# Wider first loads, a split last tile, and a re-weighted list schedule in a sparse attention and mixture-of-experts kernel

## The chip, the cores and the metric

One core of a Trainium2 chip runs the whole kernel. The metric is device time in microseconds (us) of one execution; less is better. Before the change the kernel took 168.26 us (median of three runs, 168.03 to 168.26). Engines are called PE (TensorE), VectorE (DVE in the profile), ScalarE (ACT), GpSimd (POOL) and SyncE (SP).

A profile has one execution and lists a span, which is some 1.6 us shorter than the time of the same execution (164.5 and 166.12 us in the kernel before). Each run carries a state, fast or slow. On one core "slow" means only that the run was more than 1.5% above the fastest run of the same kernel.

## The reference, cut to what matters

Four batches of 768 rows with eight heads of 64 columns go through a sparse attention (a window of 16 positions on each side, and 24 block summaries). The result, pooled over its rows, picks one of eight experts per batch; all rows of the batch then go through that expert's two layers. The code is shortened.

```python
def _attn_ref(q, k, v):                       # 4 x 8 x 768 x 64
    k_sum = k.reshape(B, H, nb, 32, D).max(axis=3)
    v_sum = v.reshape(B, H, nb, 32, D).mean(axis=3)
    scores_l = scale * q @ k.T                # kept where |i - j| < 16
    scores_s = scale * q @ k_sum.T + log(32)
    a = softmax(concat([scores_l, scores_s]))
    return a @ concat([v, v_sum])

def _moe_ref(x, w_gate, w1, w2):              # x: 4 x 768 x 512
    logits = x.mean(axis=1) @ w_gate
    e_idx = np.argmax(logits, axis=1)         # ONE expert per batch
    ...
    h = np.maximum(x[mask] @ w1[e], 0.0)      # 512 -> 1024
    out[mask] = gate_w * (h @ w2[e])          # 1024 -> 512
```

What matters is the chain of dependences: no expert weights can be loaded for a batch before all of its attention is done and its gate has been evaluated. For batch 0 this chain stands alone at the start of the program.

## The kernel before

The kernel is written as a list of operations with assumed durations. A list scheduler (`Plan`) runs over them when the program is built, gives each a start time, an engine and buffers, and then emits the instructions in that order. At each step it takes, from the operations that could start within 0.03 us of the earliest, the one with the least priority number.

```python
class Plan:
    LAT = {"pe": 0.27, "act": 0.1, "dve": 0.1, "pool": 0.1, "q": 1.6, "sp": 0.1}
    def solve(self):
        # ... for each operation whose dependences are placed: earliest start, engine, buffers
                found.append((pick[1], op.prio, op.idx, pick[0], pick[2], op, ats, room))
        # ...
            st, _, _, end, eng, op, ats, room = min(
                (c for c in found if c[0] <= smin + 0.03), key=lambda c: (c[1], c[2]))
            op.spare = st - max(room, free.get(eng, 0.0))
```

Two helpers give PE products of zeros to do at the start. `first_warm` is the first thing that PE does; `warm` puts fillers in front of an operation that the plan has waiting. They are meant to keep PE's clock up.

```python
    def warm(op, tile_):
        if op.start < WARM_UNTIL:                    # 60 us
            for _ in range(int((op.spare - 0.1) / 0.17)):
                nc.tensor.matmul(tile_, lhsT=zb[:, 0:128], rhs=zb[:, 0:HB], ...)

    def first_warm(op):
        ps = one_pool.tile([128, 512], FP32, name="wps", ...)
        for _ in range(9):
            nc.tensor.matmul(ps, lhsT=zb[:, 0:128], rhs=zb, start=True, stop=True)
```

The attention of a pair of heads is, on PE: transposes of k and q (`tps`), the scores of a half pair (`sc`, 12 to 16 small matmuls), the block sums of v (`vsps`), the product with v (`ops`), and the transpose of the result (`xps`). There is a single score buffer (`"sc": 1`). The gate's matmul is `lgps`; the expert's layers are H (`hps`) and Y (`o_ps`). The first loads, and the order of the later ones:

```python
    loads_kq(0, "k", [0], 0.8, KQ)                   # one pair of heads: 192 KB
    R["ident"] = add(("pool", 1.7), constants, 0, [last[0]])   # identity and four iotas
    for pr in ALLP:
        if pr:
            loads_kq(0, "k", [pr], 0.7, KQ)
        loads_kq(0, "q", [pr], 0.7, KQ)
        if pr == 1:
            loads_v(0, [0, 1], 2.2, VV)
    loads_v(0, [2, 3], 2.2, VV)
    # ...
    ORDER = ["kq1", "v1", "w0", "kq2", "v2", "w1", "kq3", "v3", "w2", "w3"]
```

`kq1` and `v1` are batch 1's inputs, `w0` is batch 0's gate with the loads of its expert's weights.

The softmax here doesn't subtract the row's maximum and nothing guards it: scores larger than these inputs give would overflow.

## Time and profile before

| Kernel before | Value |
|---|---|
| median of 3 runs | 168.26 us |
| profiled run | 166.12 us, span 164.5 us, mean PE clock 0.957 |
| first H matmul (steady PE work begins) | 44.99 us |
| last PE work ends, last store lands | 160.28 us, 163.11 us |

Note that the profiled run was 2 us quicker than the timed ones of the same kernel.

### The profile page before, as it was taken

The numbers are of one execution on the slowest core, as the hardware profiler recorded it, in microseconds if no ns is written. First come the engines' busy times: TensorE is split into PE (matmuls) and PEld (weight loads), VectorE is DVE, ScalarE is ACT, GpSimd is POOL, SyncE is SP. The second block draws the span as 40 slices with busy tenths as digits, with TensorE's granted clock in tenths as the row PEclk, the third lists the DMA queues.
The fourth block names the chain that finished last, engine by engine and source line by source line (L and its number), as shares of the span: only waits on it lengthen the run. The fifth ranks groups of instructions, "written<-read, shape, count | busy, mean of one in ns | idle before, by whom it ended". The sixth has DMA issues, their size and how long they took to land.

```text
span 164.5 us, 5002 instructions
## 1 busy us (share of the span) xinstructions
PE 148.9 (91%) x2136; PEld 88.0 (53%) x2136; DVE 96.9 (59%) x264; ACT 99.7 (61%) x199; POOL 46.5 (28%) x63
## 2 busy tenths in 40 slices
PE   6986989952999999999999999999999999799990
PEld 2445856741666666546556656457565445355440
DVE  5892997794498878776987588549963101000000
ACT  3174584983278766975867678469675435653341
POOL 6998600007950000697000046000000280000000
PEclk9996599995599999999999999999999999999999
DMA  3999999999999999999999999999500099990333
GB/s 32 128 137 187 164 176 210 161 133 91 162 189 206 209 176 138 102 135 262 255 234 207 194 149 144 249 257 248 113 0 0 35 165 194 277 213 12 128 128 128
DMA packets 60037, 26.01 MB, mean 158 GB/s; under 512 B 42608, under 2 KB 56944, under 8 KB 60016
## 3 DMA queue, kind: packets, MB, share of 16 engines
q0 software_dynamic: 56032, 19.40, 130.3%
q1 hardware_dynamic: 3984, 6.31, 11.3%
q8 instruction: 16, 0.26, 0.7%
q14 instruction: 5, 0.04, 0.1%
HBM read 38.81 MB, written 6.29 MB: 274 GB/s over the span
## 4 chain that ended last, share of the span: by engine, by line
PE 65%; DMA 15%; POOL 6%; DVE 6%; issue 4%; ACT 1%; POOLq 0%; ACTq 0%
PE hps L661 23%; PE o_ps L689 19%; DMA vblk<-in_v_dram 8%; DMA w_sb<-in_moe_w_dram 7%; PE tps L355 5%; PE sc L481 4%; PE ops L511 4%; PE xps L543 3%; PE vsps L426 2%; DVE vblk L447 2%; POOL k_nat L191 2%; POOL q_nat L191 1%; POOL vblk L202 1%; PE vsps L722 1%; DVE kmx L383 1%
## 5 line engine op out<-in xcount | busy, mean ns | idle before, releaser
L661 PE MATMUL hps<-xT,w_sb 128*128 128x384 bf16 x256 | 47.7, 327 | 1.4 <-DMA w_sb<-in_moe_w_dram 1.4
L689 PE MATMUL o_ps<-w_sb,hT 128*128 128x512 bf16 x192 | 44.4, 380 | 0.0
L623 POOL DMA_DIRECT2D w_sb<-in_moe_w_dram x16 | 12.0, 763 | 85.8 <-DVE kaug L402 37.8
L496 ACT ACTIVATE aT<-sc 128x768 bf16<-128x768 f32 x32 | 25.9, 808 | 11.8 <-PE sc L481 11.7
L680 ACT ACTIVATE hT<-hps 128x384 bf16<-128x384 f32 x45 | 22.1, 491 | 15.1 <-PE hps L661 14.9
L661 PEld LDWEIGHTS <-w_sb 128*128 128x128 bf16 x256 | 22.8, 98 | 15.1 <-DMA w_sb<-in_moe_w_dram 2.2
L689 PEld LDWEIGHTS <-hT 128*128 128x128 bf16 x192 | 17.4, 98 | 19.6
L708 ACT ACTIVATE o_sb<-o_ps,gcol 128x512 f32<-128x512 f32 x22 | 15.1, 687 | 16.2 <-PE o_ps L689 13.4
L528 DVE TENSOR_TENSOR xs<-ops,rv 128x384 bf16<-128x384 f32 x32 | 17.8, 558 | 1.1
L678 DVE TENSOR_SCALAR hT<-hps 128x384 bf16<-128x384 f32 x19 | 10.6, 556 | 12.1 <-PE hps L661 12.0
L552 ACT ACTIVATE xT<-xps 128x384 bf16<-128x384 bf16 x32 | 15.6, 491 | 1.2 <-PE xps L543 1.0
L202 POOL DMA_DIRECT2D vblk<-in_v_dram x10 | 15.8, 1587 | 1.4 <-DMA w_sb<-in_moe_w_dram 1.0
L481 PE MATMUL sc<-qT,kaug 64*128 64x64 bf16 x384 | 12.1, 198 | 4.6 <-issue 2.6
L317 DVE TENSOR_TENSOR aT<-aT,seen 96x768 bf16<-96x768 bf16 x24 | 12.9, 546 | 4.0 <-ACT aT L496 4.0
L383 DVE TENSOR_REDUCE kmx<-kaug 128x24 bf16<-128x768 bf16 x16 | 14.8, 932 | 0.3 <-ACT kaug L365 0.3
L365 ACT COPY kaug<-tps 128x768 bf16<-128x768 bf16 x13 | 10.0, 795 | 7.8 <-PE tps L355 7.8
L481 PEld LDWEIGHTS <-kaug 64*128 64x128 bf16 x384 | 8.3, 99 | 10.8 <-issue 7.5
L447 DVE COPY vblk<-vs_sb 24x1536 bf16<-24x1536 bf16 x16 | 12.1, 753 | 2.6 <-ACT vs_sb L365 2.2
L543 PE MATMUL xps<-identb,xs 128*128 128x128 bf16 x96 | 10.7, 220 | 0.6 <-DVE xs L528 0.6
L365 ACT COPY qT<-tps 128x768 bf16<-128x768 bf16 x13 | 9.9, 798 | 2.1 <-PE tps L355 2.0
L511 PEld LDWEIGHTS <-aT 120*64 120x64 bf16 x384 | 8.4, 117 | 5.0 <-issue 3.4
L511 PE MATMUL ops<-vblk,aT 120*64 120x65 bf16 x384 | 10.4, 203 | 0.3 <-DVE vblk L447 0.3
(89 smaller groups left out, 145.8 us busy)
## 6 DMA issues: line engine op xcount, KB each, us to landing
w_sb<-in_moe_w_dram POOLq DMA_DIRECT2D x12, 512.0 KB, 13.4
out_dram<-o_sb SPq DMA_DIRECT2D x24, 256.0 KB, 5.9
vblk<-in_v_dram POOLq DMA_DIRECT2D x6, 576.0 KB, 22.2
k_nat<-in_k_dram POOLq DMA_DIRECT2D x3, 768.0 KB, 14.5
q_nat<-in_q_dram POOLq DMA_DIRECT2D x3, 768.0 KB, 17.6
vblk<-in_v_dram POOLq DMA_DIRECT2D x2, 564.0 KB, 18.4
w_sb<-in_moe_w_dram POOLq DMA_DIRECT2D x8, 128.0 KB, 4.5
w_sb<-in_moe_w_dram POOLq DMA_DIRECT2D x4, 256.0 KB, 7.7
```

Of the source, the lines that this page charges most:

```text
L202: nc.gpsimd.dma_start(vb[p0:p1, n0:n1, 0:D], bass.AP(v.tensor, v.offset + ((b * H * NJ + n0) * QB - HALO + p0) * D, [[D, p1 - p0], [QB * D ...
L365: nc.scalar.copy(out_, in_)
L383: nc.vector.tensor_reduce(out=kmxs[b, pr].rearrange("q (j c) -> q j c", c=QB // BLK), in_=kaugs[b % 2][:, pr, :, R_OWN:R_POST].rearrange(" ...
L481: nc.tensor.matmul(sc[:, hh, w * QB : (w + 1) * QB], lhsT=ka[rs, pr, j, :], rhs=qT[rs, j * QB : (j + 1) * QB], start=b > 0 and w == 0, sto ...
L496: nc.scalar.activation(aT, scs.pop((b, pr, u))[:, :, 0:HB], ACT.Exp, scale=SCALE)
L511: nc.tensor.matmul(ops[w * QB : (w + 1) * QB, t, hh, :], lhsT=aT[0:NR, hh, c0 : c0 + QB], rhs=vb[0:NR, 2 * pr + hh, u * NW + 2 * t + w, 0 ...
L528: nc.vector.tensor_tensor(out=xs, in0=ops[:, :, :, 0:D], in1=rv.unsqueeze(3).to_broadcast([128, NW // 2, 2, D]), op=ALU.mult,)
L543: nc.tensor.transpose(xps[:, t * 128 : (t + 1) * 128], xs[:, t], identb)
L552: nc.scalar.activation(xT[b][:, pr, u * HB : (u + 1) * HB], xpss.pop((b, pr, u)), ACT.Copy, accum_out=red[b][:, pr, u : u + 1],)
L661: nc.tensor.matmul(hps[:, 0:HB], lhsT=w1_sb[:, dt, ft * 128 : (ft + 1) * 128], rhs=xT[b][:, dt, u * HB : (u + 1) * HB], start=(dt == 0), s ...
L680: nc.scalar.activation(dst, hps[:, 0:HB], ACT.Relu)
L689: nc.tensor.matmul(o_ps, lhsT=hTs[b][:, ft, st * 128 : (st + 1) * 128], rhs=wts[b][1][:, ft, :], start=(ft == 0), stop=(ft == NFT - 1),)
```

## The change

The intent has three parts. (1) *Loads*: batch 0's k and q come in four transfers of two pairs of heads instead of eight of one, v last, and the identity is built early, apart from the other constants. (2) *Halves*: the last 128 rows of the output are computed, evicted and stored as two halves of 256 columns, so that what follows PE's last matmul is shorter. (3) *Plan*: urgencies per kind of operation are added to the priorities, found by a search in which the model's durations were disturbed; and the plan gets a term for the fetching of PE's instructions, a block of 256 usable `FETCH` us after the block before was entered.

```diff
+    FETCH = 4.5
+    SLACK = 0.03
+    URGENCY = {
+        "Vs": 3, "gb": 155, "mul": 100, "vo": -37, "xo": -99, "qo": 4, "Tq": 4,
+        "kmx": 7, "S": -20, "rest": -4, "exp": -120, "own": -113, "X": 6, "H": 152,
+        "ho": 152, "gc": 152, "Y": 152, "yo": 152,
+    }
     ... [solve; the rest of it keeps a list of ready operations, with the same choice]
+                if op.count:
+                    r = max(r, come.get((done + op.count) // block, 0.0))
-                found.append((pick[1], op.prio, op.idx, ...
+                found.append((pick[1], op.prio + self.URGENCY.get(op.kind, 0.0), op.idx, ...
+            if op.count:
+                if (done + op.count) // block > done // block:
+                    come[(done + op.count) // block + 1] = end + self.FETCH
+                done += op.count
     ... [halves]
+    def Z_mm(b, st, c):      # o_ps[:, 0:256] = hT x w2[:, c-th half], 8 matmuls
+    def Z_out(b, st, c):     # evicts 256 columns and issues its own store
-        for st in range(NST):
+        for st in range(NST - (b == B - 1)):
+        if b == B - 1:
+            for c in range(2):
+                ...
+                m = add(("pe", 0.9), Z_mm(b, NST - 1, c), "Y", base + 20 + c, ...)
+                o = add(EITHER(0.45, 0.5), Z_out(b, NST - 1, c), "yo", base - 165, [m, gc])
     ... [loads]
+    FIRST = "k01 i0 q01 k23 i1 q23 v01 v23".split()
-    loads_kq(0, "k", [0], 0.8, KQ)
-    ... [the loop shown above]
+    for what in FIRST:
+        if what[0] == "i":
+            R["ident", int(what[1])] = ... (identity, constants)[int(what[1])] ...
+        elif what[0] == "v":
+            loads_v(0, [int(c) for c in what[1:]], 2.2, VV)
+        else:
+            loads_kq(0, what[0], [int(c) for c in what[1:]], 0.7, KQ)
     ... [every add() gets a kind; PE's also a count of instructions; the plan's time for a v load goes from 2.15 to 2.25]
```

The arithmetic is unchanged.

## The prediction

> **What bounds the kernel now.** The program runs on one core, so I went straight to the page's 40 slices, then summed three stretches, then read the chain of waits and the waits list. Slices (each 4.1 us; tenths of a slice) first:

> ```profile
> PE   6986989952999999999999999999999999799990
> PEclk9996599995599999999999999999999999999999
> DMA  3999999999999999999999999999500099990333
> ```

> From slice 12 on TensorE (PE) is full, at full clock, but for one dip near slice 35; before that it is patchy, and its granted clock falls twice. The sums (columns: stretch, length, then busy us and count per engine, clock, DMA share, GB/s):

> ```profile
> 0.00:44.50 44.50, 34.86 (x687) 23.08 (x689) 32.27 (x99) 24.93 (x44) 23.93 (x39) 0.85 1.85 143
> 44.50:160.00 115.50, 113.80 (x1464) 64.88 (x1452) 64.59 (x165) 73.91 (x154) 22.53 (x25) 1.00 1.30 166
> 160.00:164.50 4.50, 0.28 (x2) 0.00 (x0) 0.00 (x0) 0.88 (x2) 0.00 (x0) 0.94 0.31 117
> ```

> So three regimes: 44.5 us of start, 115.5 us in which PE is busy for 113.8, and 4.5 us of tail. In the middle the order of instructions can gain almost nothing except the idle 1.7 us. The waits list names most of it, and the other stall that matters:

> ```profile
> PE sc L481 <- issue: 2.6, 1, 2.6
> PE hps L661 <- DMA w_sb<-in_moe_w_dram: 1.4, 1, 1.4
> ```

> The second is the last batch's first weights, late at 144.1. The first lies in the start; the chain of waits shows where (columns: start us, length, what):

> ```profile
> 10.76 13.98 DMA vblk<-in_v_dram
> 24.78 0.86 PE vsps L426 x24
> ...
> 34.97 0.35 PE lgps L576 x8
> ...
> 35.43 0.23 PE sc L481 x4
> 35.67 2.64 issue
> 38.31 0.41 PE sc L481 x8
> ```

> The start hangs on the second half of batch 0's v, landed at 24.74 (10.76 + 13.98), then on 10 us of attention work up to the gate's matmul (lgps, 34.97), then on the gate's weights. Those are issued at 37.88 and land from 42.30. The last v of batch 1 landed at 40.14, just ahead of them: in this trace the loads land nearly in issue order, so the weights stand behind 1.5 MB of k and q and 1.15 MB of v of batch 1. Steady PE work begins at 44.7 to 45.0.

> [...]a fetch packet starts at 35.38 and takes 1.54 us, and PE stands still from 35.67 to 38.31 with nothing to wait for. I read this stall as that fetch; no run yet proves it. [...]the records show 0.5 from 13.7 to 20.6, after the thin stretch 11 to 15, and again from 37.6 to 44.5, right after the stall. [...]The last six stores of 256 KB land 2.0 us after issue[...].

> **The change part by part.**

> First loads. Eight issues of one pair of heads (192 KB; k and q, four pairs) become four of two pairs (384 KB), and the eye matrix is built before the four iotas instead of with them. GpSimd pays 0.63 us for each such issue (median of the k_nat and q_nat rows early on), so 4 x 0.63 = 2.5 us less. Today k0's 192 KB are alone in the queue from 2.24 to 4.59, when q0's issue ends: the engines have little to do until then. After, 384 KB are queued by 2.3, the next 384 KB by about 3.6 (0.6 us of identity plus 0.75 us of issue). v's two halves go to the end, issued at about 6.4 to 8.8 and 8.8 to 10.6. The bytes before the end of batch 0's v are the same 2.7 MB, only fed sooner: I take 2 us (between 1.5 and 2.7) off v's last landing, 24.7 to about 22.7, and off everything behind it: batch 1's last v from 40.1 to about 38. The first half of v lands later (15.0 today, about 17 to 19 then), the k and q of pairs 2 and 3 much earlier (15.6 to 19.5 today, about 10 to 12 then). That is a good exchange: scores need k and q only, eight of them fit the nine aT buffers, and so ScalarE's 8 x 0.81 us of exp and 8 x 0.80 us of copies can be done before the last v. The first transpose starts later (384 KB in place of 192 KB at some 190 GB/s: +1.0 us on 5.34) but is not on the path: VectorE's constants occupy it to 6.8 today and set the first maximum.

> The last rows. The last 128 rows go as two halves of 256 columns: 16 matmuls instead of 8. Three transposes of 128 columns with their weight loads take 0.17 us, 0.056 each, so 256 columns should take 0.11: 16 x 0.11 = 1.76 us against 8 x 0.218 = 1.75. PE breaks even. The last eviction, 0.69 us for 512 columns, falls to about 0.45 (384 columns take 0.49), and the store loses perhaps 0.2 of its 2.0. Sum: -0.4 us, all on the path.

> Urgencies, slack and the fetch model. They change no arithmetic, only order, ScalarE or VectorE, buffers and the fillers[...]. H, Y and their evictions fall by 152, that is behind the attention of the next two batches, which so ends earlier; the gate of the last batch follows, and with it the last weights: I count half of the 1.4 us wait, -0.7. The model spreads PE's instructions so that a block of 256 is not used up within 4.5 us of its fetch. If that removes the 2.64 us stall, the half clock after it goes too. What it is worth: steady work could begin when the first weights land. They are issued after attention 0 (about 2 us sooner from v, about 1 more from less VectorE and ScalarE work left after v) and must land behind batch 1's v (about 38): at 40 to 41 instead of 42.3, and PE takes them at once rather than at 45.0. Steady work begins up to 4 us earlier; I count 3, as the fillers and a new order will not hit it exactly. Against this +0.2 us for stalls at new places.

> Sum: -3.0 - 0.7 - 0.4 + 0.2 = -3.9 us of 168.26, to 164.4 us.

> **The rivals.** (a) *The weights' landing sets the steady start.* If DMA is saturated from 6 us on whatever the order (its row shows 9 in slices 2 to 28), the loads gain only their first idle microsecond, and the change is worth 1 + 0.7 + 0.4, about 2 us: 166.2. For: the row of nines. Against: today PE starts 2.7 us after the weights are there. (b) *Fetch stalls move.* Drawn together, attention uses 24 or 32 instructions per 0.3 to 0.45 us, a block in some 4 us; today's late fetch cost more than the modelled 4.5 us[...]. Two new stalls of 2.6 us with half clock after them eat the gain: 168 to 169. Against: the search has this term, and today's steady stretch shows no such gap. (c) *All of it works*: weights at 39, four more score groups done before them (4 x 0.28), no wait for the last weights: -6 -1 -1.4 -0.5 with some loss, 160 to 161. For: ScalarE and VectorE are busy only 25 and 32 us of the first 44.5. Against: such plans meet real durations that the model has not.

> **Range and chances.** Rival (a) at 166.2 and the full success at 160.5 lie on both sides of 164.4; the profiled run of before took 166.1 and the timed ones 168.0 to 168.3, so the start varies by 2 us on its own. Range 160.8 to 167.4. The 2% line is 164.9, close to my centre: faster 0.57, within 2% 0.40, slower 0.03, since nothing adds work to the saturated middle.

> **What would show it.** Right: k and q of all pairs landed by 12 to 13 us; batch 0's v by 23; the gate's matmul at 31 to 33; no PE issue gap over 1 us in the first 45 us, and no half clock after 21; first H matmul at 40 to 42; the busy sum of the steady part unchanged within 2 us; the last eviction at 0.45 us; the wait for the last weights under 0.7. Wrong: v's landing unmoved (then rival a), a new issue gap followed by clock 0.5 (rival b), or PE idle between the early attention and the weights, which would say that landing alone sets the start.

## More of the kernel before

From the profile's costliest groups (busy us, mean ns of one, idle before) and its table of queues (packets, MB, share):

```profile
L661 PE MATMUL hps<-xT,w_sb 128*128 128x384 bf16 x256 | 47.7, 327 | 1.4 <-DMA w_sb<-in_moe_w_dram 1.4
L689 PE MATMUL o_ps<-w_sb,hT 128*128 128x512 bf16 x192 | 44.4, 380 | 0.0
q8 instruction: 16, 0.26, 0.7%
```

The two layers alone are 92 us of PE work, which no order of instructions makes smaller.

## The result, and the profile after

| | before | changed |
|---|---|---|
| runs | 168.26, 168.03, 168.26, 167.20 | 165.29, 165.71, 165.48, 165.85 |
| median | 168.14 us | 165.59 us |
| profiled run: time, span | 166.12, 164.5 us | 165.29, 163.6 us |

The ratio is 0.986 (95% interval 0.982 to 0.990), within the 2% that counts as the same. A ratio is the mean time of one kernel's fast runs over the mean of the other's of the same rounds, so it is not quite the ratio of the medians quoted. A repetition on another chip (below, after_again) gave 0.996 (0.990 to 1.003). So the two estimates of the gain are 1.4 and 0.4%, and the second is not clear of nothing.

The same views as the prediction read, for the changed kernel: the slices, then the three stretches (cut at the same 44.5 and 160 us).

```profile
PE   6797789694498999999999999998999999999991
PEclk9999999759569999999999999999999999999999
DMA  2999999991999999999999999999500099993333
```

```profile
0.00:44.50 44.50, 33.73 (x662) 22.22 (x663) 33.44 (x101) 24.43 (x44) 19.32 (x32) 0.88 1.97 133
44.50:160.00 115.50, 114.18 (x1486) 66.23 (x1480) 67.06 (x168) 72.40 (x151) 25.03 (x28) 0.99 1.34 170
160.00:163.60 3.60, 0.02 (x1) 0.00 (x0) 0.00 (x0) 0.47 (x1) 0.00 (x0) 0.99 0.32 114
```

The dip near slice 35 is gone, and the stretch after 160 us is 0.9 us shorter (PE's own end came 0.26 us of that sooner). But the start is as long as it was: PE is full from slice 12 on, no sooner, and the low clock has moved, from slices 4 to 5 and 10 to 11 to slices 8 to 9 and 11 to 12. The chain of waits through the start of the changed kernel (start us, length, what) says why:

```profile
28.77 0.18 PE ops L537 x4
28.95 1.62 issue
30.57 0.43 PE ops L537 x8
...
32.86 1.39 PE xps L780 x4
...
35.22 2.08 PE tps L381 x47
37.30 0.02 issue
37.32 0.96 DVE qT L393
...
40.01 0.36 PE sc L507 x12
```

The stall of 2.64 us that stood at 35.67 in the kernel before has become one of 1.62 us at 28.95, in the middle of a group of 12 matmuls that had begun, with nothing to wait for. It no longer stands behind the gate but in front of it. Then come four fillers (L780), and batch 1's transposes, the last 64 of them of q, and only then the gate's matmul, at 37.58 instead of 34.97. The records give the half clock from 30.39 to 37.22 and from 40.63 to 47.46. Two stretches of 3.41 us, each just before such a fall, from the sums by stretch of the changed kernel (length, then PE's busy time and count first; the clock is third from the end):

```profile
26.98:30.39 3.41, 1.97 (x64) 1.48 (x54) 2.50 (x6) 2.55 (x6) 0.00 (x0) 1.00 2.17 169
30.39:33.80 3.41, 3.23 (x47) 2.29 (x48) 2.51 (x4) 1.27 (x3) 0.00 (x0) 0.50 4.35 136
37.22:40.63 3.41, 1.54 (x50) 1.10 (x47) 3.24 (x12) 2.43 (x6) 0.31 (x1) 1.00 0.09 8
```

A 3.41 us stretch in which PE was busy for 1.97 us was followed by half clock; so was one with 1.54. In the first, all the idle time is the stall. (The half clock of each of these two falls lasted 6.83 us, and so it did at the two falls of the kernel before in its start; a stretch is half of that, and the full clock between the changed kernel's two spells lasted just 3.41 us.) But so short a stall was not always followed by half clock. I cut all 14 traces into such stretches, in step with the clock's own changes: of those at full clock, every one with PE busy for less than 1.8 us was followed by half clock (18 of the 25 falls), and none with more than 2.3 us was. Between these it went either way: in before_shift128, 33.01 to 36.42 us with 1.82 us busy was not followed by half clock, and 36.42 to 39.83 with 2.30 was.

**Where the time of the profiled pair went.** I counted PE's useful work, each kind of matmul at the time that it takes at full clock, fillers left out: 123.4 us in all. (The times per kind are my estimate from the traces; with other reasonable ones the total is up to 128 us, and one kernel shifts against another by 0.2 to 0.5 us. Smaller differences of this count are not to be read.) The first 16 us of it are done at 44.31 us before and at 44.51 after. So the start gained nothing. At 30 us of useful work the changed kernel is 1.9 us behind (61.50 against 59.63; its first layers ran at half clock to 47.46), at 60 us of it 1.0 behind, at 104 us of it 1.5 behind. Only then, where the wait for the last batch's weights stood, does it catch up, making good 1.75 us: at 122 us of work it is 0.3 ahead. The tail, from PE's end to the last landing, is 2.83 us before and 2.33 after. Net: 0.77 us between the last landings (163.11 and 162.34). The timed difference of 2.5 us is larger because the profiled run of before was one of its quick ones.

### The profile page after: what moved, and what is told of

The parts are those of the page before. It is cut to its first block, busy times and chain, and to the rows that moved or that the text cites. A ratio compares the mean times of both kernels' runs of the same rounds, so it can differ in the third digit from the quotient of the medians.

```text
span 163.6 us, 5016 instructions
## 1 busy us (share of the span) xinstructions
PE 147.9 (90%) x2139; PEld 88.5 (54%) x2139; DVE 100.5 (61%) x268; ACT 97.3 (59%) x196; POOL 44.3 (27%) x59
## 4 chain that ended last, share of the span: by engine, by line
PE 79%; DVE 10%; ACT 3%; DMA 3%; issue 2%; ACTq 0%; POOLq 0%
PE o_ps L715 25%; PE hps L687 25%; PE tps L381 8%; PE xps L569 4%; PE sc L507 4%; PE ops L537 4%; DVE vblk L473 4%; DMA k_nat<-in_k_dram 3%; PE vsps L452 2%; PE tps L780 2%; ACT aT L522 2%; DVE qT L393 1%; DVE kmx L409 1%; PE o_ps L744 1%; PE xps L780 1%
## 5 line engine op out<-in xcount | busy, mean ns | idle before, releaser
L715 PE MATMUL o_ps<-w_sb,hT 128*128 128x512 bf16 x184 | 43.5, 380 | 0.0
L687 PEld LDWEIGHTS <-w_sb 128*128 128x128 bf16 x256 | 23.5, 98 | 13.4 <-issue 0.5
L706 ACT ACTIVATE hT<-hps 128x384 bf16<-128x384 f32 x44 | 21.2, 490 | 12.1 <-PE hps L687 11.6
L715 PEld LDWEIGHTS <-hT 128*128 128x128 bf16 x184 | 16.4, 98 | 17.7
L734 ACT ACTIVATE o_sb<-o_ps,gcol 128x512 f32<-128x512 f32 x19 | 13.1, 687 | 16.2 <-PE o_ps L715 12.9
L343 DVE TENSOR_TENSOR aT<-aT,seen 96x768 bf16<-96x768 bf16 x24 | 12.3, 550 | 4.1 <-ACT aT L522 4.0
L537 PE MATMUL ops<-vblk,aT 120*64 120x65 bf16 x384 | 9.8, 198 | 3.4 <-DVE vblk L473 1.8
L391 ACT COPY kaug<-tps 128x768 bf16<-128x768 bf16 x11 | 8.4, 797 | 6.3 <-PE tps L381 6.3
L473 DVE COPY vblk<-vs_sb 24x1536 bf16<-24x1536 bf16 x16 | 11.6, 725 | 0.7 <-ACT vs_sb L391 0.3
L537 PEld LDWEIGHTS <-aT 120*64 120x64 bf16 x384 | 7.9, 112 | 7.0 <-issue 4.2
```

Source lines behind the costliest of these rows:

```text
L391: nc.scalar.copy(out_, in_)
L473: nc.vector.tensor_copy(vblks[b % NV][R_SUM:NR, 2 * pr : 2 * pr + 2, :, 0:D], vss[b, pr][BLK * pr : BLK * pr + NB] .unsqueeze(2) .to_broad ...
L537: nc.tensor.matmul(ops[w * QB : (w + 1) * QB, t, hh, :], lhsT=aT[0:NR, hh, c0 : c0 + QB], rhs=vb[0:NR, 2 * pr + hh, u * NW + 2 * t + w, 0 ...
L687: nc.tensor.matmul(hps[:, 0:HB], lhsT=w1_sb[:, dt, ft * 128 : (ft + 1) * 128], rhs=xT[b][:, dt, u * HB : (u + 1) * HB], start=(dt == 0), s ...
L706: nc.scalar.activation(dst, hps[:, 0:HB], ACT.Relu)
L715: nc.tensor.matmul(o_ps, lhsT=hTs[b][:, ft, st * 128 : (st + 1) * 128], rhs=wts[b][1][:, ft, :], start=(ft == 0), stop=(ft == NFT - 1),)
```

## The experiments

All kernels gave correct results. "Mark" is the time at which the first 16 us of useful PE work are done. "before" in a row of times means the kernel before, run in the same rounds. By the 2% rule no run has a verdict other than "same" or "unclear" on record (unclear: after_again, gate_first, hold_v1 and shift256; none for shift128). So what follows rests on the intervals and, above all, on the traces.

### The parts one at a time

Theory A: the loads and the plan act on the start and each gives a part of the gain. Rival B: the start is set by when PE's instructions come, so the parts show nothing there, and what remains is the tail and the last weights.

**halves_only**: the kernel before with the halves alone.

```diff
-        for st in range(NST):
+        for st in range(NST - (b == B - 1)):
...
+        if b == B - 1:
+            for c in range(2):
+                ... Z_mm and Z_out as in the change, no urgencies
```

> The kernel before plus only the two half stores at the end; its first 150 us are the same instructions, so its trace is also a second look at the start of the kernel before. Tail theory: the span loses the 0.7 to 0.8 us that the last landing moved (163.11 to 162.34 in the two traces), so the time is 0.5 to 0.8 us under the kernel before, ratio 0.995 to 0.997. Rival: sixteen matmuls of 256 columns cost PE what the smaller store saves, ratio 0.999 to 1.001. Its start should show a PE issue gap at recorded instruction 1217 (mod 256 = 193) if the gap is the instruction fetch.

Measured: 166.55 us median (165.45 to 167.92) against 166.84 for before (11 runs, four of them slow), ratio 1.002 (0.996 to 1.009). From PE's end to the last landing it took 2.34 us, not 2.83. The stall in the start is where it was, from PE's part of the timeline (start, length, engine line op; in brackets the idle time before):

```profile
38.09 0.40 PE L481 MATMUL sc<-qT,kaug 64*128 64x64 bf16 x8 [2.42 <-issue]
```

So the halves are worth 0.5 us at the end of the trace, too little to show in six runs that scatter over 2.5 us: the times decide for neither expectation. The stall is at 1217, as expected.

**loads_only**: the kernel before with the new first loads alone.

```diff
-    loads_kq(0, "k", [0], 0.8, KQ)
-    ... [old loop]
+    FIRST = "k01 i0 q01 k23 i1 q23 v01 v23".split()
+    for what in FIRST: ... [as in the change]
```

> The kernel before plus only the two-pair first loads and the split constants; no urgencies, no halves. Theory A (loads move data 2 us sooner, but instruction fetch and the half clock after it hold the gate back): the last v of batch 0 lands at 22 to 23, yet the gate's matmul stays at 33 to 37 and the time gains 0 to 1.2 us (ratio 0.993 to 1.000). Rival B (the loads are the gain): ratio 0.982 to 0.988, as the whole change.

Measured: 166.28 us (165.60 to 167.26), ratio 1.000 (0.995 to 1.006). Batch 0's last v landed at 23.5 instead of 24.74 and batch 1's at 38.72 instead of 40.14, so the data came 1.2 and 1.4 us sooner. PE did not profit. Its timeline:

```profile
35.87 0.29 PE L578 MATMUL lgps<-wg_sb,reds 128*1 128x8 f32 x6 [0.24 <-DVE reds L569]
39.21 0.19 PE L578 MATMUL lgps<-wg_sb,reds 128*1 128x8 f32 x2 [3.05 <-issue]
44.95 1.46 PE L663 MATMUL hps<-xT,w_sb 128*128 128x384 bf16 x4
```

Here the stall cuts the gate's own eight matmuls in two, so that the first weights land only at 44.78 (42.30 before). Steady work begins at 44.95, as before. In this order the weights' landing does come just ahead of the steady start.

**no_urgency**: the changed kernel with `URGENCY = {}`.

```diff
-    URGENCY = {"Vs": 3, "gb": 155, ...}
+    URGENCY = {}
```

> The whole change without the table of urgencies (empty), so with the new first loads, the halves and the fetch term. Theory A (what the whole change gains after the start comes from the urgencies, by the last batch's weights being issued or needed at a better time): the PE wait for the last weights is back at 1 us or more, and the time is 0.8 to 2 us over the whole change (ratio to before 0.991 to 0.998). Rival B (loads and halves carry it all): ratio 0.984 to 0.988, wait or not.

Measured: 166.12 us (165.17 to 166.41), ratio 0.997 (0.992 to 1.002). A stall of 3.57 us ended at 38.88, with the gate's matmul behind it. The time is in the range of Theory A, but its mechanism, that the wait for the last batch's weights comes back, was a miss. PE's last H work has no such wait:

```profile
140.81 5.39 PE L683 MATMUL hps<-xT,w_sb 128*128 128x384 bf16 x32
```

The wait is 1.4 us in the kernel before, 1.3 in halves_only and 1.0 in before_shift128; it is 0 in the changed kernel, 0.39 in after_again, and 0 in loads_only (less than 0.05) and old_first too. So in these traces, one of each, it went with the new loads under the old plan and with the urgencies under the old loads; the urgencies are not needed for it.

**old_first**: the changed kernel with the old order of the first loads.

```diff
-    FIRST = "k01 i0 q01 k23 i1 q23 v01 v23".split()
+    FIRST = "k0 i0 i1 q0 k1 q1 v01 k2 q2 k3 q3 v23".split()
```

> The whole change with the first loads put back to one pair each, in the old order, and the identity with the other constants. Theory A (first loads worth little once the fetch holds the gate): ratio to before 0.984 to 0.992. Rival B (they are most of the gain): ratio 0.994 or more. The last v of batch 0 should land at 24 to 25 again.

Measured: 167.60 us (166.12 to 169.54, two of six slow), ratio 1.004 (0.996 to 1.012). The last v of batch 0 and 1 landed at 25.31 and 40.17, the mark came at 45.89 us, 1.4 us after the changed kernel's 44.51. This is what Rival B expected (0.994 or more): under the new plan the loads appear to be worth something, 0.8% by after_again and 1.8% by the first comparison, although loads_only shows nothing under the old plan. The interval here overlaps that of after_again and not that of the first comparison (0.982 to 0.990); those were on other chips, and I don't call it shown.

What follows from the four: all lie within 0.4% of the kernel before. For halves_only and loads_only that is what the part is worth alone; no_urgency and old_first leave a part out, and would have to be set against the changed kernel. In all of them PE stood still once for 2.4 to 3.6 us in the start with nothing to wait for.

**after_again**: the changed kernel, unaltered, on another chip.

> The changed kernel unaltered, timed again on the chip of this batch, because the kernel before spread over 165.2 to 169.9 us in 11 runs of the last batch and the first comparison had 4 runs of each. Theory A (the start of every variant is held by the instruction fetch, so the change is small): ratio to before 0.988 to 0.997, with the changed kernel's runs closer together (range under 1.5 us). Rival B (the first comparison stands): 0.982 to 0.988.

Measured: 166.16 us (165.60 to 167.28) against 167.53 (165.64 to 170.51, 11 runs, four slow), ratio 0.996 (0.990 to 1.003), as Theory A expected. Its stalls were 1.90 and 1.21 us, its mark 44.71 us.

### What the stalls have in common

I counted PE's recorded instructions, matmuls and weight loads together with the few records of its sequencer (9 or 10, waits and drains), in order of time. In every trace, each stall of 0.2 us or more in the start (after the first microsecond) that the profile puts down to "issue" stands at number 705, 961 or 1217 of that count (the first has number 0), each 256 after the one before. Longer idle times at other numbers all have a releaser with a name: a transfer, VectorE, or the exponential that frees the score buffer. What stands there differs: a score group, the product with v, the gate, a transpose of q. The number does not. (The first boundary in this count is at 193, not 256; the records don't show what fills the rest of the first block.) Each boundary has a packet on the instruction queue (q8, 16 KB each). For each boundary: when PE entered the block, when the packet for the next block started and how long it took, when PE entered the next block, PE's idle time there, and the DMA share from the entry to the packet's start:

| kernel, block | entered | packet starts, takes | next block entered | idle there | DMA share, entry to packet |
|---|---|---|---|---|---|
| before, 705 | 25.71 | 28.57, 0.97 | 30.90 | none | 1.26 |
| before, 961 | 30.90 | 35.38, 1.54 | 38.30 | 2.64 | 3.77 |
| before, 1217 | 38.30 | 39.36, 1.52 | 46.74 | none | 0.41 |
| changed, 449 | 18.36 | 22.02, 1.07 | 24.38 | 0.22 | 2.82 |
| changed, 705 | 24.38 | 28.19, 0.96 | 30.57 | 1.62 | 1.39 |
| changed, 961 | 30.57 | 35.23, 1.64 | 38.51 | 0.43 | 4.59 |
| changed, 1217 | 38.51 | 39.54, 0.91 | 48.74 | none | 0.00 |

In every row the packet for the next block started only after PE had entered the present one. It started 2.9 to 4.7 us later in the rows up to 961, among the start's loads (DMA share 1.26 to 4.59), and 1.0 to 1.1 us later at 38 us, when few of them or none were still under way (0.41 before, 0.00 changed). It took 0.9 to 1.6 us, and PE entered the next block 1.3 to 1.6 us after that, save in the rows of 1217, where PE was not there yet. So in the other five rows 256 instructions (128 matmuls with their weight loads) took 5.2 to 7.9 us. (The share alone does not give the delay: later in the changed kernel, blocks were entered at 48.74 and 57.12 us and the packets started 1.20 us after, at DMA shares of 1.22 and 1.28.) The attention work is made of small matmuls, which by the prediction's estimate would use up a block in some 4 us: in the changed kernel PE stood idle at three boundaries in a row (0.22, 1.62 and 0.43 us), in the kernel before only at the last (2.64 us). **Theory C**: up to 38 us the fetches, which start late among the loads, set when the start ends. Theory A lives on as its rival: the start is a chain of data and dependences, and the stalls sit in slack.

### Two tests of the order

**gate_first**: the gate's matmul of batch 0 ahead of batch 1's q transposes.

```diff
         gs.users.append(p)
+        if b == 0:
+            for pr in ALLP:
+                R["Tq", 1, pr].deps.append(m)
```

> The whole change, plus the plan's rule that batch 1's q transposes (64 transposes, 128 PE instructions) come after batch 0's gate matmul instead of before it. Theory A (the gate's matmul is held by fetch blocks and half clock in front of it): the gate's matmul runs at 33.0 to 35.5 instead of 37.6, inside the block that starts at recorded instruction 961, and the first weights are issued by 38 instead of 40.3; the next stall is again at recorded instruction 1217. The time gains 0 to 1.5 us, as the S groups still wait for that block. Rival B (the gate is held by ScalarE and VectorE): its matmul stays after 36.5.

Measured: 167.66 us (165.83 to 168.80, one of six slow), ratio 1.001 (0.993 to 1.009). PE's timeline:

```profile
34.88 0.35 PE L602 MATMUL lgps<-wg_sb,reds 128*1 128x8 f32 x8 [0.87 <-DVE reds L593]
38.99 0.39 PE L507 MATMUL sc<-qT,kaug 64*128 64x64 bf16 x7 [2.09 <-issue]
45.47 1.46 PE L687 MATMUL hps<-xT,w_sb 128*128 128x384 bf16 x4
```

The gate came 2.7 us sooner than in the changed kernel, and its first weights landed at 41.06 instead of 43.36. Steady work began 0.6 us sooner and the mark did not move (44.47 against 44.51), because the next boundary (38.98) now stood behind the gate, with the score groups still to come behind it, each some 1.4 to 1.5 us after the one before through the single score buffer. So the chain through the gate, which I took for the start's critical path in the prediction, is not alone. Whether the fetch at 38.98 or the score groups behind it bind more, this run does not separate.

**hold_v1**: batch 1's v loaded after batch 0's weights, so that few loads are under way at one boundary.

```diff
-    ORDER = ["kq1", "v1", "w0", "kq2", "v2", ...]
+    ORDER = ["kq1", "w0", "v1", "kq2", "v2", ...]
```

> The whole change, but batch 1's v is loaded after batch 0's first weights instead of before them; up to the gate's matmul PE's order is the same as in the changed kernel. Theory A (an instruction block waits in the DMA queues behind the bulk loads): with no v of batch 1 in the queues the fetch packet for the block at recorded instruction 1217 starts within 2 us of PE entering the block at 961 (4.7 us in the changed kernel), and no issue gap over 0.5 us is left at 1217; first weights land by 42. The whole may be slower by 0 to 4 us, since DMA idles from 30 to 40. Rival B (a block takes 6 to 8 us whatever the load): packet 4 us or more after entry, gap kept.

Measured: 173.79 us (172.24 to 176.01, one of four slow), ratio 1.046 (1.035 to 1.056). The time is worse, but it is the start that this run was for. First the sums by stretch (the last two numbers are DMA share and GB/s), each from the entry to block 961 to the start of the next packet: for the changed kernel, then for hold_v1.

```profile
30.57:35.23 4.66, 4.66 (x54) 2.93 (x56) 2.57 (x5) 1.85 (x5) 0.00 (x0) 0.50 4.59 134
```

```profile
29.87:30.93 1.06, 1.06 (x36) 0.89 (x37) 0.66 (x2) 0.41 (x2) 0.00 (x0) 1.00 0.08 15
```

Next hold_v1's PE timeline, and its sums over the stretch that follows.

```profile
29.87 0.32 PE L537 MATMUL ops<-vblk,aT 120*64 120x65 bf16 x8 [0.80 <-issue]
32.44 1.55 PE L381 MATMUL tps<-identb,q_nat 96*64 96x96 bf16 x64
33.92 0.35 PE L602 MATMUL lgps<-wg_sb,reds 128*1 128x8 f32 x8
34.20 0.35 PE L507 MATMUL sc<-qT,kaug 64*128 64x64 bf16 x12
40.53 0.85 PE L687 MATMUL hps<-xT,w_sb 128*128 128x384 bf16 x2
```

```profile
41.00:100.00 59.00, 52.76 (x780) 32.12 (x779) 35.44 (x89) 34.53 (x74) 19.55 (x18) 0.86 1.76 174
```

The DMA share was 0.08 and not 4.59 (it adds up the times of packets that overlap, so it can pass 1), and the packet started 1.06 us after the entry, not 4.66. It took 1.38 us, and block 1217 was entered at 34.24 without any idle time, 4.3 us sooner than in the changed kernel. Steady work began at 40.53 and the mark came at 40.85, 3.7 us sooner. So with the loads taken away the delay went too. The 3.7 us need not all be the fetch's: the gate's stretch also ran at full clock here (1.00 against 0.50 in the two lines above), and the weights, too, had no v of batch 1 ahead of them. The loss of the gain goes with something else: batch 1's v now landed at 62.62 instead of 38.45, and PE was busy for 52.8 of the 59 us from 41 to 100 (56.2 in the changed kernel), with half clock from 74.5 to 88.2.

### Moving the boundaries against the work

If the fetch chain sets the start, it should pay to start it sooner. The opening fillers take 4 us for 9 matmuls. The same 4 us of fillers in smaller pieces would use up half a block more, and every later boundary would be reached earlier in time and in the work.

**shift128**: 73 small opening matmuls instead of 9 large ones, 128 more instructions in the same time.

```diff
-        for _ in range(9):
-            nc.tensor.matmul(ps, lhsT=zb[:, 0:128], rhs=zb, start=True, stop=True)
+        for _ in range(73):
+            nc.tensor.matmul(ps[:, 0:64], lhsT=zb[:, 0:128], rhs=zb[:, 0:64], start=True, stop=True)
```

> The whole change with the nine opening warm-up matmuls of 512 columns replaced by 73 of 64 columns: the same PE time, 128 PE instructions more. Theory A (the issue gaps are block boundaries of 256 instructions): gaps stay at recorded instruction numbers with remainder 193 of 256 (705, 961, 1217), so they fall on work 128 instructions earlier in the program's order. Rival B (the gaps belong to the work, e.g. an unseen wait before that O group or S group): they stay at the same work and their numbers move to remainder 65. Time within 1.5 us of the changed kernel.

Measured: 163.71, 163.37, 166.41 and 165.87 us. Two of the four are slow against the lowest; the mean of all four is 164.8, against 166.2 for after_again. The opening took 4.07 us instead of 4.02. Block 449 was entered at 14.10 instead of 18.36, block 1217 at 34.53 instead of 38.51. The stall at 1217 stands in the q transposes now:

```profile
32.17 0.45 PE L381 MATMUL tps<-identb,q_nat 96*64 96x96 bf16 x12
34.53 1.30 PE L381 MATMUL tps<-identb,q_nat 96*64 96x96 bf16 x52 [1.91 <-issue]
35.75 0.34 PE L602 MATMUL lgps<-wg_sb,reds 128*1 128x8 f32 x8
44.43 1.46 PE L687 MATMUL hps<-xT,w_sb 128*128 128x384 bf16 x4
```

The place moved as the count of instructions says, by 128 instructions of work, and not with the work: that settles that these stalls belong to the blocks. The mark came at 42.86 us, 1.7 us sooner than the changed kernel, and PE's end 1.6 us sooner (158.43 against 160.02).

**shift128_again**: the same kernel with six runs on another chip.

> shift128 unaltered, timed again with more rounds, as its four runs split 163.4 to 163.7 and 165.9 to 166.4. Theory A (128 more small instructions at the start bring the fetch chain forward and take one of the two stalls away): ratio of fast runs to before 0.980 to 0.990, PE stalls at 961 and 1217 together under 2.5 us, steady work a microsecond or more earlier than in the changed kernel. Rival B (chance): ratio 0.993 to 1.000, as after_again.

Measured: 164.71 us (163.71 to 165.79) against 166.73 for before (165.75 to 168.60), ratio 0.989 (0.983 to 0.995). Mark 42.62, PE's end 158.82. The gain in the trace repeats. By its median and PE's end this is the best kernel. After the changed kernel's 0.996 and 0.986, its own lead over the changed kernel rests on the traces and on the four runs of shift128. The expectation that the stalls shrink (together under 2.5 us) was a miss:

```profile
27.00 0.32 PE L507 MATMUL sc<-qT,kaug 64*128 64x64 bf16 x10 [0.82 <-issue]
34.29 1.30 PE L381 MATMUL tps<-identb,q_nat 96*64 96x96 bf16 x52 [2.30 <-issue]
```

These 3.12 us are as much as after_again's 3.11, and still the mark is 2.1 us sooner. So the gain is not a smaller sum of stalls. What differs is that in both traces of shift128 the clock stays full up to the gate (half clock from 37.00 and 35.69 us, the gate at 35.75 and 35.51), while in the changed kernel's two traces part of the work before the gate ran at half clock. That this is where the gain comes from is not shown.

**shift128_gate**: shift128 with the edit of gate_first.

> shift128 plus the rule of gate_first. Theory A (with the fetch ahead, the gate's matmul and the first weights become what the steady start waits for): the gate's matmul at 32 to 34 (35.75 in shift128), weights landed by 40.5, time 0.3 to 1.5 us under shift128's 164.8. Rival B (the S groups, one per 1.46 us through the single score buffer at half clock, set the start): the gate earlier, the first H matmul still at 44 to 45, no gain, 164 to 166.

Measured: 165.87 us (163.79 to 166.94, one of six slow), ratio 0.996 (0.988 to 1.004). The gate came at 31.96 us and the first H at 43.24, both sooner than in shift128, and the mark at 42.24. But PE ended at 160.46, not at 158.43. The two edits do not add up; where the 2 us went after the mark I did not trace.

**shift256**: a whole block more, 137 opening matmuls of 34 columns.

```diff
-        for _ in range(9):
-            nc.tensor.matmul(ps, lhsT=zb[:, 0:128], rhs=zb, start=True, stop=True)
+        for _ in range(137):
+            nc.tensor.matmul(ps[0:64, 0:34], lhsT=zb[:, 0:64], rhs=zb[:, 0:34], start=True, stop=True)
```

> As shift128 but with 137 small opening matmuls (34 columns, 64 weight columns): 256 PE instructions more than the changed kernel, so the block boundaries lie at the same work as there, one block number later. Theory A (the fetch is a chain, one block per 6 to 8 us under load, and an earlier start of the chain is what shift128 gained): PE enters the block at recorded instruction 193 at about 3 us and the one at 449 before 9 us, the stalls at 1217 (the old 961 work) and 1473 shrink below 1 us together, and the time is 163 to 165.5, under the changed kernel. Rival B (what counts is only where the boundaries lie relative to the work): stalls and time as in the changed kernel, 165.5 to 166.5.

Measured: 169.51 us (168.52 to 170.25), ratio 1.019 (1.014 to 1.025). This is a miss by its construction. From PE's timeline:

```profile
1.33 7.49 PE L788 MATMUL wps<-zb 128*64 128x34 bf16 x137 [1.33 <-DVE vblk L247]
```

The opening took 7.49 us, 55 ns for each pair of matmul and weight load, no less than with 64 columns (4.07 us / 73 = 56 ns). I had assumed that fewer columns cost less. The weight loads had 64 columns here and 128 in shift128, so neither count shows in the 55 and 56 ns; what sets them is not shown. The first real transposes came at 9.18 instead of 6.51 us, and the stalls at 961 and 1217 were 0.64 and 2.72 us; the run says nothing about a shift of a whole block.

**before_shift128**: the kernel before with the opening of shift128.

```diff
-        for _ in range(9): ...
+        for _ in range(73): ...        # as in shift128, in the kernel before
```

> The kernel before with the same opening as shift128 and nothing else. Theory A (the fetch chain held the kernel before as well): its stall of 2.4 to 2.6 us at recorded instruction 1217 moves to work 128 instructions earlier and is smaller or partly hidden, ratio 0.985 to 0.997. Rival B (the old plan is bound elsewhere at the start): 0.998 to 1.005.

Measured: 168.89 us (166.68 to 172.68, two of six slow), ratio 1.009 (1.000 to 1.017), above what either theory expected. No gain, if anything a loss:

```profile
37.05 0.53 PE L355 MATMUL tps<-identb,q_nat 96*64 96x96 bf16 x16 [2.22 <-issue]
38.72 0.34 PE L576 MATMUL lgps<-wg_sb,reds 128*1 128x8 f32 x8
```

In the kernel before, the boundary stood just behind the gate. Moved by 128 instructions, it came to stand in front of it, and the gate fell from 34.97 to 38.72 us. So smaller opening matmuls are not good in themselves: the same opening had a ratio of 0.989 under the changed plan (shift128_again) and of 1.009 here. Here the loss in the start went with the work that the boundary stood in front of; how far that holds for other orders is not shown.

### What the starts have in common

| kernel | block 1217 entered | first H | mark | PE ends |
|---|---|---|---|---|
| before | 38.30 | 44.99 | 44.31 | 160.28 |
| changed | 38.51 | 46.08 | 44.51 | 160.02 |
| after_again | 38.84 | 46.28 | 44.71 | 160.76 |
| halves_only | 38.09 | 44.57 | 43.97 | 160.16 |
| loads_only | 39.21 | 44.95 | 43.94 | 160.25 |
| no_urgency | 38.88 | 45.83 | 44.83 | 160.89 |
| old_first | 40.12 | 47.46 | 45.89 | 161.41 |
| gate_first | 38.98 | 45.47 | 44.47 | 161.98 |
| hold_v1 | 34.24 | 40.53 | 40.85 | 166.93 |
| shift128 | 34.53 | 44.43 | 42.86 | 158.43 |

In the first eight, which have the same opening and the same loads in the queues at that point, the mark follows block 1217 by 4.7 to 6.0 us, whatever was done to the order or the first loads. From the mark to PE's end is 115.5 to 117.5 us in all but hold_v1. The time is thus the start plus a nearly fixed rest, and the start of the first eight is the entry to block 1217 plus some 5 to 6 us. That is a likeness of eight starts which differ by 2 us, not a proof. The two runs that moved the block are the test: against the changed kernel it came 4.3 (hold_v1) and 4.0 us (shift128) sooner, and the mark 3.7 and 1.7 us.

The plan's own fetch term was a separate question, answered by building alone, without a run. With `FETCH = 0` the changed plan gives the same order of instructions on every engine: the term is without effect. Two reasons can be read off. Its 4.5 us are less than the 5.2 to 7.9 us measured; with 6.0 in its place the order does change, also seen by building alone. And it counts only the planned instructions, not the fillers, so that its boundaries are not where the real ones are.

## Why the prediction was right or wrong

The time, 165.59 us, lies inside the range and 1.2 us above the centre. The forecast leaned to "faster" (0.57); what came, "within 2%", had 0.40. The steps behind it fared unevenly, and that the sum came close is in part luck, as shown below the list.

1. *The loads' landings*: right. Batch 0's v landed at 22.78 (forecast 22.7), batch 1's last at 38.45 (38), and all k and q by 12.20 (12 to 13).
2. *"Steady work begins up to 4 us earlier; I count 3"*: this is the step that failed. The first H came at 46.08, not at 40 to 42, and 1.1 us later than before; by the mark the start lost 0.2 us, within the error of that count. The gate came at 37.58, not at 31 to 33. The 3 us assumed that the model's term would take the 2.64 us stall and its half clock away, and that data arriving sooner would then be used sooner. The runs showed that the term is without effect, that the stall only moved (1.62 us at 28.95, then half clock from 30.39), and that the fetches had not moved: block 1217 was entered at 38.51 against 38.30. With few loads under way at one boundary (hold_v1, DMA share 0.08), steady work did begin at 40.53. So the size was real, but the change had no hold on it.
3. *Rival (b), "Fetch stalls move"*: this was the right account of the start. I gave it too little weight, partly because "the search has this term". It also overstated the outcome: at 168 to 169 it reckoned with two stalls of 2.6 us, and there were 1.62, 0.43 and 0.22.
4. *Rivals (a) and (c)*: rival (a) came out near the measured time (166.2), but for another reason. The weights were not what PE waited for in the kernel before (2.7 us between landing and use), and gate_first, with weights 2.3 us sooner, did not move the mark. Rival (c) is excluded for this kernel.
5. *The wait for the last weights, -0.7*: too small, and for the wrong reason. It fell from 1.4 us to nothing in the profiled run (0.39 in after_again), so -1.0 to -1.4. The prediction gave this to the urgencies; the wait is gone without them too (no_urgency, loads_only).
6. *The tail, -0.4*: right. The last eviction took 0.47 us (forecast 0.45) in place of 0.69, the halved store landed 1.7 to 1.8 us after issue in place of 2.0, and from PE's end to the last landing it went from 2.83 to 2.33 us. All traces with halves that I compared for it have 2.3, those without 2.8.
7. *The fetch reading itself*, of which the prediction said "no run yet proves it": shown, by the count of 256 in every trace, by shift128 (the stall moved with the count and not with the work) and by hold_v1 (with the loads gone the packet started 1.06 us after the entry, not 4.66, and the idle time at 1217 was none, not 0.43).
8. *The clock's fall "right after the stall"*: the records have it at 37.63 us, while the stall lasted from 35.67 to 38.31, so it came within the stall. PE was busy for 0.96 of the 3.41 us before.

The sum came out near the measured time by luck: a missing 3 us in the start stood against a baseline at 168.3 that was itself in the upper half of what this kernel does: in 48 runs, 13 of them slow, before took 164.8 to 170.5 us. In this scatter the changed kernel's ten runs took 165.3 to 167.3 us.

What stays open: how much each part is worth alone, since all lie within the noise of some 0.7%; why the runs of before scatter more than the changed kernel's; why shift128 gained, with stalls no smaller; why shift128_gate lost after its mark; how far the single score buffer, whose groups follow one another by 1.4 to 1.5 us before the first H, sets the start beside the fetches (no run had two buffers); and whether an opening between 9 and 73 matmuls, or a plan with a correct fetch term, would do better.
